# Moving the subtraction that makes a weight's low part from VectorE to GpSimd, in a one-core attention and feed-forward kernel

## The chip, the cores and the metric

The kernel runs on one core of one Trainium2 chip. The metric is the device time of one execution in microseconds. The engines are named as in the profile: PE is TensorE's matrix multiplication and PEld its weight load, DVE is VectorE, ACT is ScalarE, POOL is GpSimd and SP is SyncE, which here only issues DMAs.

## The reference

Eight batches of 448 tokens go through attention with 12 heads of 64 (q and k are first normalised by their root mean square and scaled by a gain), then through a two-dimensional Fourier transform whose real part is added to the input, and then through a feed-forward layer over 768 and 3072 columns. Cut to what is computed:

```python
q_n, k_n = rmsnorm(q, g_q), rmsnorm(k, g_k)
attn = softmax(q_n @ k_n.T / 8)
x = (attn @ v)                      # heads side by side: [8, 448, 768]
u = x + real(fft2(x))               # over tokens and columns
un = (u - mean(u)) / sqrt(var(u) + 1e-06)
out = u + relu(un @ w_ch1) @ w_ch2
```

The two weight matrices come as 64-bit floats; everything else is 32-bit.

## The kernel before, in words

PE multiplies numbers in a rounded 32-bit format (F32R in the code). To keep precision, an operand is held as two such numbers: a high part, which is the value rounded, and a low part, which is the value less its high part. A product of two split operands takes three passes.

`ffn` is the main stream: for each batch, `up(m)` multiplies with piece m of the first weight matrix (24 pieces of 6 blocks of 128x128, so 768 columns, tile h on line 992), and `down(g, d)` with piece (g, d) of the second one (36 pieces of 4 blocks, 512 columns, tile o on line 1013). The pieces' split form sits in tiles w, in two streams with three tiles each, which alternate in the first batch.

In the first batch no split form exists yet, and `convert` makes it from the 64-bit weights, once for each of the 60 pieces; afterwards the split form is stored to DRAM (line 793) and later batches only load it. Its steps for one piece, with the lines of the profile:

- line 746: SP loads the 64-bit words into a tile dbl (two buffers, which a few other tiles share).
- lines 749 and 750, ACT: the absolute value of each word's high half goes to a tile mag (two buffers); the low half is scaled in place.
- lines 751, 755 and 759, DVE: a clamp, a shift and a bit merge on mag, the last one with dbl as its second input.
- line 763, POOL: mag plus the low half of dbl, as 32-bit integers. It is the last reader of dbl.
- line 764, ACT: the rounded value goes to w's high part.
- line 765, DVE: mag less the high part goes to w's low part. It is the last reader of mag.

Fourteen of the pieces are converted early, while the attention of the first batches runs, and their tiles are called mage, dble, w1e and w2e; the other 46 are converted as the first batch's `ffn` comes to need them (mag, dbl, w).

Around this runs the side stream `aux`: attention of a batch (`transpose_pair`, `softmax_pair`, `value_pair`), the folding of its output for the Fourier transform (`fold`, tiles eo, sd and tot on DVE), the transform itself (`spectral`, tiles y, Y, ab, smdf, x and un). For the first batch it has PE to itself, for later ones it is merged into the `ffn` of the batch before. POOL's other work is a power of -1/2 on a small tile ss, which each head pair's normalisation waits for; a copy rs for the division by the softmax sums in the first two batches; the same power for rstd; and, from the third batch on, the squares qkn.

Each engine runs its instructions in order. That order is written by the framework's scheduler, which plans the whole program with its own estimate of each instruction's length; a change of one instruction's engine can so change the order on all of them. `behind` adds one rule: while the first batch's attention runs, a conversion step is placed no earlier than four recorded instructions back on its engine. Small operations that all go through one helper have its line, 114, so they are told apart by their tiles.

Of the kernel before, what the change touches and what calls it, by code (L numbers as in the profile page):

```python
# [11 lines left out]
F32 = mybir.dt.float32  # L12
# [4 lines left out]
ALU = mybir.AluOpType  # L17
# [73 lines left out]
def spectral_block(ctx, tc, q, k, v, g_q, g_k, w1, w2, d1, d2, out, nb=B):  # L91
    nc = tc.nc
# [30 lines left out]
    def order(ins, before, kind, reason):  # L123
        tc.add_manual_dep(
            ins.ins, before.ins.name, mybir.DependencyInfo(kind, reason),
            reason="issue order",
        )

    def behind(ins):

        others = given.get(ins.ins.engine, [])
        if starting[0] and len(others) > LAG:
            order(
                ins, others[-1 - LAG],
                mybir.DependencyClass.NoSync, mybir.DependencyReason.DATA,
            )
# [23 lines left out]
    def wide(name, dtype=F32):  # L160
        return sb.tile([128, 1800], dtype, tag="X", name=name, bufs=2)
# [576 lines left out]
    def convert(src, bits, part, name):  # L738

        _, c, f = src.shape
        raw = wide(f"dbl{name}", U32)[:, : c * f].rearrange(
            "r (c f w) -> r c f w", c=c, w=2
        )
        nc.sync.dma_start(raw.rearrange("r c f w -> r c (f w)"), src)
        low, high = raw[:, :, :, 0], raw[:, :, :, 1]
        value = bits.bitcast(F32)
        behind(nc.scalar.activation(value, high.bitcast(F32), AF.Abs))
        behind(nc.scalar.activation(low, low, AF.Copy, scale=2.0**-29))  # L750
        behind(nc.vector.tensor_scalar(
            out=value, in0=value, scalar1=MIN_HIGH, scalar2=MAX_HIGH,
            op0=ALU.max, op1=ALU.min,
        ))
        behind(nc.vector.tensor_scalar(
            out=bits, in0=bits, scalar1=5, scalar2=2,
            op0=ALU.logical_shift_left, op1=ALU.logical_shift_right,
        ))
        behind(nc.vector.scalar_tensor_tensor(  # L759
            out=bits, in0=high, scalar=0xC0000000, in1=bits,  # L760
            op0=ALU.bitwise_and, op1=ALU.bitwise_or,
        ))
        behind(nc.gpsimd.tensor_tensor(out=bits, in0=bits, in1=low, op=ALU.add))  # L763
        behind(nc.scalar.copy(part[0], value))
        behind(nc.vector.tensor_tensor(
            out=part[1], in0=value, in1=part[0], op=ALU.subtract
        ))

    early = set()
# [1 line left out]
    class Stream:  # L771
# [14 lines left out]
        def converted(self, p, name):  # L786
            hl = self.tile(p, name)
            n = hl.shape[2]
            bits = slot("M", f"mag{name}", U32)[:, : n * 128].rearrange(
                "r (c f) -> r c f", c=n  # L790
            )
            convert(piece_doubles(p), bits, [hl[:, k] for k in range(2)], name)
            nc.sync.dma_start(piece_kept(p), hl.bitcast(F32))
            return hl
# [314 lines left out]
```

## Time and profile before

| what | value |
|---|---|
| median of 3 runs | 2173.51 us |
| the runs | 2165.72, 2174.75, 2173.51 us |
| span of the profiled execution | 2158.8 us |
| its own device time | not listed apart; the lowest run is 6.9 us above the span |
| granted TensorE clock, mean over the span | 0.983 |
| PE, DVE, ACT, POOL busy | 2085.6, 1551.6, 1053.9, 343.4 us |

The span reaches from the first to the last instruction that the profile holds. The busy times are sums over the whole span; what they mean for one stretch is read from a table by stretches.

### The profile page before, as it was taken

What the parts mean: (1) busy time and instruction counts of PE and PEld (TensorE: products, weight loads), DVE (VectorE), ACT (ScalarE), POOL (GpSimd) and SP (SyncE); (2) the same over time, 40 slices, a digit from 0 to 9 for tenths busy, and PEclk for the clock granted to TensorE, in tenths of its full rate; (3) what the DMA queues carried; (4) which work ended last, traced back from release to release, by engine and by line L of the source; (5) the groups of instructions that cost most, each with busy time, mean ns of one, the idle gap of its engine ahead of it and who ended that gap; (6) DMA issues with size and microseconds to landing.
All of it is one profiled execution on the core that took longest, in us unless ns stands there. A gap on an engine that the chain in (4) does not pass through costs nothing.

```text
span 2158.8 us, 31384 instructions
## 1 busy us (share of the span) xinstructions
PE 2085.6 (97%) x11224; PEld 1858.1 (86%) x11224; DVE 1551.6 (72%) x3016; ACT 1053.9 (49%) x2258; POOL 343.4 (16%) x196
## 2 busy tenths in 40 slices
PE   7878999899999999999999999999999999999998
PEld 4557788788999999999999999999999989999998
DVE  7888788877885788758786688857787578754122
ACT  7967776455552555435552455425553355422100
POOL 4323334311110111001110011101110011000000
PEclk8977999999999999999999999999999999999999
DMA  5548877757555855667555666558556674458774
GB/s 172 181 125 272 257 249 255 243 200 214 170 167 182 238 180 168 175 206 225 161 176 177 215 197 176 171 190 239 171 165 188 204 209 142 150 175 251 234 248 150
DMA packets 294976, 424.79 MB, mean 197 GB/s; under 512 B 183283, under 2 KB 221156, under 8 KB 294820
## 3 DMA queue, kind: packets, MB, share of 16 engines
q1 hardware_dynamic: 290386, 420.67, 63.5%
q10 hardware_dynamic: 4434, 2.11, 0.4%
q8 instruction: 89, 1.46, 0.3%
q14 instruction: 67, 0.55, 0.1%
HBM read 362.53 MB, written 65.31 MB: 198 GB/s over the span
## 4 chain that ended last, share of the span: by engine, by line
PE 77%; DMA 3%; DVE 3%; ACT 1%; issue 1%; POOL 0%; DVEq 0%; SPq 0%; POOLq 0%; ACTq 0%
PE h L992 28%; PE o L1013 28%; PE S L382 5%; PE av L492 4%; PE pt L480 4%; DMA dbl<-w 2%; PE y L617 1%; PE qk L334 1%; PE oT L949 1%; PE x L649 1%; PE un L861 1%; PE av L497 1%; PE ab L694 1%; PE rem L437 1%; DMA u_dram<-u 1%
## 5 line engine op out<-in xcount | busy, mean ns | idle before, releaser
L1013 PE MATMUL o<-hs,w 128*128 128x448 f32 x3456 | 793.2, 372 | 2.9 <-DVE rounded L114 0.9
L992 PE MATMUL h<-unT,w 128*128 128x448 f32 x3456 | 784.0, 371 | 1.0 <-DVE hs L114 0.6
L1013 PEld LDWEIGHTS o<-hs,w 128*128 128x128 f32 x3456 | 638.4, 188 | 60.5 <-issue 3.8
L992 PEld LDWEIGHTS h<-unT,w 128*128 128x128 f32 x3456 | 639.8, 189 | 57.5 <-issue 4.1
L114 ACT ACTIVATE P<-S,mn 112x448 f32<-112x448 f32 x384 | 243.9, 637 | 196.9 <-DVE mn L114 188.1
L114 DVE TENSOR_REDUCE mn<-S 112x1 f32<-112x448 f32 x384 | 233.8, 617 | 33.0 <-PE S L382 30.3
L114 ACT ACTIVATE hs<-h 128x448 fp32r<-128x448 f32 x192 | 104.4, 544 | 304.5 <-PE h L992 302.9
L114 DVE SCALAR_TENSOR_TENSOR hs<-h,hs 128x448 fp32r<-128x448 f32 x192 | 119.3, 621 | 149.3 <-ACT hs L114 147.3
L114 DVE TENSOR_TENSOR acc<-o,acc 128x448 f32<-128x448 f32 (+1 forms) x240 | 147.0, 613 | 81.8 <-PE o L1013 79.1
L114 POOL TENSOR_TENSOR qkn<-raw 112x1024 f32<-112x1024 f32 x36 | 69.2, 1924 | 677.4 <-PE qk L334 391.5
L114 POOL TENSOR_TENSOR ss<-ss,nhalf 112x16 f32<-112x16 f32 x48 | 143.6, 2992 | 205.6 <-DVE ss L114 183.6
L382 PE MATMUL S<-KD,QT 128*112 128x448 f32 x384 | 152.8, 400 | 18.5 <-ACT KD L114 15.6
L114 ACT CAST T<-pt 128x448 fp32r<-128x448 f32 x216 | 112.9, 533 | 101.5 <-PE pt L480 97.9
L492 PE MATMUL av<-T,vhl 128*128 128x448 f32 x432 | 154.2, 385 | 0.8 <-DVE T L114 0.8
L114 DVE TENSOR_TENSOR T<-pt,T 128x448 fp32r<-128x448 f32 x216 | 131.7, 617 | 25.7 <-ACT T L114 24.7
L382 PE MATMUL S<-rounded,QT 128*112 128x448 f32 x384 | 143.7, 376 | 0.0
L114 DVE TENSOR_SCALAR P<-P,sm 112x448 f32<-112x448 f32 x288 | 122.7, 465 | 3.9
L480 PE MATMUL pt<-ident,P 112*128 112x112 f32 x864 | 122.1, 258 | 0.0
L480 PEld LDWEIGHTS pt<-ident,P 112*128 112x128 f32 x864 | 102.7, 140 | 15.8
L763 POOL TENSOR_TENSOR mag<-mag,dbl 128x512 uint32<-128x512 uint32 (+1 forms) x46 | 77.6, 1686 | 170.3 <-DVE mag L759 115.2
L114 POOL TENSOR_TENSOR rstd<-st,nhalf 112x1 f32<-112x1 f32 (+2 forms) x32 | 18.2, 570 | 505.7 <-DVE st L114 500.1
L382 PEld LDWEIGHTS S<-KD,QT 128*112 128x112 f32 x384 | 68.5, 179 | 29.4 <-ACT KD L114 18.7
(116 smaller groups left out, 2528.3 us busy)
## 6 DMA issues: line engine op xcount, KB each, us to landing
w<-w SPq DMA_DIRECT2D x192, 768.0 KB, 5.4
w<-w SPq DMA_DIRECT2D x288, 512.0 KB, 4.5
dbl<-w SPq DMA_DIRECT2D x28, 512.0 KB, 5.3
dbl<-w SPq DMA_DIRECT2D x18, 768.0 KB, 5.1
raw<-q SPq DMA_DIRECT2D x96, 112.0 KB, 3.9
raw<-k SPq DMA_DIRECT2D x96, 112.0 KB, 4.0
v<-v SPq DMA_DIRECT2D x96, 96.0 KB, 3.6
u_dram<-u SPq DMA_DIRECT2D x24, 336.0 KB, 3.1
```

The costliest lines, as they stand in the source:

```text
L114: ins = emit(*args, **kwargs)
L334: nc.tensor.transpose(pt[:, c * C : (c + 1) * C], qk[:, i, c].rearrange("t h d -> t (h d)"), ident[:C, :C],)
L382: ins = nc.tensor.matmul(s_, QT[:, h, cs], K[:, h], start=step == 0, stop=step == 1)
L437: nc.tensor.transpose(rem[:, c * C : (c + 1) * C], Pc[c][:, 384:512], ident[:C, :C])
L480: nc.tensor.transpose(pt[:, c * C : (c + 1) * C], Pc[c][:, 512 * h + j * 128 : 512 * h + (j + 1) * 128], ident[:C, :C],)
L492: nc.tensor.matmul(av[:, :S], lv, T[:, i], start=(j == 0 and i == 0), stop=False)
L497: nc.tensor.matmul(av[:, :S], lv, R[:, h], start=False, stop=True)
L617: nc.tensor.matmul(o, src[:, par, t0 : t0 + n], D1[:, ri, par, cols], start=i != 1, stop=i != 0,)
L649: nc.tensor.transpose(xp[:n, i * 128 : (i + 1) * 128], src[:, 3 * half + i], ident)
L763: behind(nc.gpsimd.tensor_tensor(out=bits, in0=bits, in1=low, op=ALU.add))
L992: pace(nc.tensor.matmul(o, w[:, a, c], unT[c][:, z], start=n == 0, stop=n == 17))
L1013: pace(nc.tensor.matmul(o, w[:, a, f], hs[4 * g + f][:, z], start=n == 0, stop=n == 11))
```

## The change

The subtraction on line 765 is issued to GpSimd. Its second input is read as a plain 32-bit float; the numbers are the same bits.

```diff
--- before.py
+++ after.py
@@ -762,8 +762,8 @@
         ))
         behind(nc.gpsimd.tensor_tensor(out=bits, in0=bits, in1=low, op=ALU.add))
         behind(nc.scalar.copy(part[0], value))
-        behind(nc.vector.tensor_tensor(
-            out=part[1], in0=value, in1=part[0], op=ALU.subtract
+        behind(nc.gpsimd.tensor_tensor(
+            out=part[1], in0=value, in1=part[0].bitcast(F32), op=ALU.subtract
         ))
 
     early = set()
```

The order of instructions moves on all engines from here to the middle of the second batch. Three places follow; lines with - stand only before, with + only after the change.

The first is on DVE, where the first batch's last head pair is divided (xT), the second batch's scores are reduced (mn) and its queries are split (QT). The tiles mage4_1 and w1e4_1 belong to the early piece (4, 1).

```order
 L755 TENSOR_SCALAR mage4_1_1274<-mage4_1_1274 128x512
+L759 SCALAR_TENSOR_TENSOR mage4_1_1274<-dble4_1_1275,mage4_1_1274 128x512
 L114 TENSOR_REDUCE mn1_0_0_1262<-S1_0_0_1_1264 112x1
-L759 SCALAR_TENSOR_TENSOR mage4_1_1274<-dble4_1_1275,mage4_1_1274 128x512
 L114 TENSOR_REDUCE mn1_0_1_1312<-S1_0_1_0_1313 112x1
-L765 TENSOR_TENSOR w1e4_1_1273<-mage4_1_1274,w1e4_1_1273 128x512
 L114 TENSOR_REDUCE mn1_0_1_1312<-S1_0_1_1_1314 112x1
+L114 TENSOR_TENSOR QT1_1_1434<-qk1_1_0_1436,QT1_1_1434 64x448 x2
+L114 TENSOR_REDUCE mn1_0_2_1371<-S1_0_2_0_1372 112x1
 L114 TENSOR_TENSOR xT0_295<-rt0_5_1388,xT0_295 128x448
```

The subtraction has left DVE's queue, the bit merge stands one reduction earlier, and the split of QT has moved ahead of the division.

The second is on DVE too, where the first batch's normalised rows are split for `ffn` (unT) and its first pieces are converted.

```order
 L114 SCALAR_TENSOR_TENSOR u0_3_1581,st0_3_1582<-x0_111_1588,smdf0_1_1547 112x384
+L114 TENSOR_SCALAR st0_3_1582<-st0_3_1582 112x1
 L751 TENSOR_SCALAR mag_0_1_1627<-mag_0_1_1627 128x768
-L114 TENSOR_SCALAR st0_3_1582<-st0_3_1582 112x1
 L755 TENSOR_SCALAR mag_0_1_1627<-mag_0_1_1627 128x768
 L759 SCALAR_TENSOR_TENSOR mag_0_1_1627<-dbl_0_1_1628,mag_0_1_1627 128x768
-L751 TENSOR_SCALAR mag_0_2_1640<-mag_0_2_1640 128x768
 L114 TENSOR_SCALAR st0_1_1564<-st0_1_1564 112x1
-L755 TENSOR_SCALAR mag_0_2_1640<-mag_0_2_1640 128x768
-L759 SCALAR_TENSOR_TENSOR mag_0_2_1640<-dbl_0_2_1641,mag_0_2_1640 128x768
 L114 TENSOR_TENSOR unT0_0_1685<-un0_0_1680,unT0_0_1685 128x448
```

Three conversion steps of piece 2 have gone from ahead of unT to behind it.

The third is on POOL, in the first batch's `ffn`, at pieces (2, 3) and (2, 4) of the second matrix; ss1_5 is the power for the second batch's last head pair.

```order
+L763 TENSOR_TENSOR mag_0_2_3_2837<-mag_0_2_3_2837,dbl_0_2_3_2838 128x512
+L763 TENSOR_TENSOR mag_0_2_4_2885<-mag_0_2_4_2885,dbl_0_2_4_2886 128x512
+L765 TENSOR_TENSOR w1_0_2_3_2836<-mag_0_2_3_2837,w1_0_2_3_2836 128x512
 L114 TENSOR_TENSOR ss1_5_3045<-ss1_5_3045,nhalf_73 112x16
-L763 TENSOR_TENSOR mag_0_2_3_2837<-mag_0_2_3_2837,dbl_0_2_3_2838 128x512
-L114 COPY rs1_2_2899<-sums1_2_2138 112x512
-L763 TENSOR_TENSOR mag_0_2_4_2885<-mag_0_2_4_2885,dbl_0_2_4_2886 128x512
+L765 TENSOR_TENSOR w2_0_2_4_2884<-mag_0_2_4_2885,w2_0_2_4_2884 128x512
```

The power ss1_5 now stands behind two integer additions and one subtraction, of which it stood ahead before; and a subtraction stands between one piece's addition and the next.

## Rows read from the trace of the kernel before

**Rows 1.** The page's head, and part 1: busy time, share, instructions of each engine.
```profile
span 2158.8 us, 31384 instructions
PE 2085.6 (97%) x11224; PEld 1858.1 (86%) x11224; DVE 1551.6 (72%) x3016; ACT 1053.9 (49%) x2258; POOL 343.4 (16%) x196
```

**Rows 2.** Busy time by stretches; the first row names the columns.
```profile
core 0: us, PE busy (x) PEld busy (x) DVE busy (x) ACT busy (x) POOL busy (x), PEclk, DMA share, GB/s
...
20.00:120.00 100.00, 80.58 (x394) 53.76 (x393) 90.11 (x154) 96.03 (x215) 40.28 (x22) 0.93 0.55 166
120.00:190.00 70.00, 47.70 (x208) 37.38 (x206) 59.66 (x116) 47.44 (x89) 21.32 (x14) 0.68 0.59 201
190.00:450.00 260.00, 247.05 (x1236) 206.57 (x1235) 213.56 (x345) 170.44 (x335) 95.83 (x56) 0.99 0.75 246
...
540.00:2158.00 1618.00, 1611.16 (x8891) 1476.93 (x8889) 1112.87 (x2238) 684.51 (x1503) 169.11 (x88) 1.00 0.63 190
```

**Rows 3.** PE's waits, 20 to 120 us: us in total, times, longest.
```profile
PE S L382 <- ACT KD L114: 9.2, 7, 3.5
```

**Rows 4.** PE's waits, 120 to 190 us.
```profile
PE un L861 <- ACT un L114: 5.0, 2, 3.6
...
PE ab L694 <- DVE smdf L114: 3.2, 1, 3.2
...
PE S L382 <- DVE QT L114: 2.6, 1, 2.6
```

**Rows 5.** PE's waits, 190 to 450 us.
```profile
PE y L617 <- DVE eo L114: 4.2, 1, 4.2
PE qk L334 <- DVE qkn L114: 2.3, 1, 2.3
```

**Rows 6.** Groups of line 765 on DVE: busy us, mean ns; idle before.
```profile
L765 DVE TENSOR_TENSOR w<-mag,w 128x512 fp32r<-128x512 f32 (+1 forms) x46 | 39.0, 848 | 7.0 <-ACT w L764 5.7 <-issue 1.0
L765 DVE TENSOR_TENSOR w2e<-mage,w2e 128x768 fp32r<-128x768 f32 (+1 forms) x7 | 5.8, 832 | 0.7 <-ACT w2e L764 0.7
L765 DVE TENSOR_TENSOR w1e<-mage,w1e 128x512 fp32r<-128x512 f32 (+1 forms) x7 | 5.3, 758 | 1.3 <-ACT w1e L764 1.3
```

**Rows 7.** POOL's groups; two lines in tile mag's view (min/median/max ns, first, last start).
```profile
L763 POOL TENSOR_TENSOR mag<-mag,dbl 128x512 uint32<-128x512 uint32 (+1 forms) x46 | 77.6, 1686 | 170.3 <-DVE mag L759 115.2 <-DMA w<-w 10.9 <-ACT mag L749 9.0
L114 POOL TENSOR_TENSOR qkn<-raw 112x1024 f32<-112x1024 f32 x36 | 69.2, 1924 | 677.4 <-PE qk L334 391.5 <-DMA w<-w 162.2 <-DVE hs L114 102.9
...
L763 POOL TENSOR_TENSOR mag<-mag,dbl x46: 1276/1540/2895, 159.3 to 447.0; 128x512 uint32<-128x512 uint32 x28, 128x768 uint32<-128x768 uint32 x18
L764 ACT CAST w<-mag x46: 603/622/865, 169.5 to 448.6; 128x512 fp32r<-128x512 f32 x28, 128x768 fp32r<-128x768 f32 x18
```

**Rows 8.** Line 755 in the view of mag, and the timeline at 370 us.
```profile
L755 DVE TENSOR_SCALAR mag<-mag x46: 407/428/2250, 157.5 to 445.6; 128x512 uint32<-128x512 uint32 x28, 128x768 uint32<-128x768 uint32 x18
...
370.51 2.25 DVE L755 TENSOR_SCALAR mag<-mag 128x768 uint32<-128x768 uint32 x1
...
369.63 2.72 POOL L114 TENSOR_TENSOR qkn<-raw 112x1024 f32<-112x1024 f32 x1 [1.94 <-PE qk L334]
```

**Rows 9.** DVE's timeline (start, length, what, idle before) at four subtractions.
```profile
135.92 0.69 DVE L765 TENSOR_TENSOR w1e<-mage,w1e 128x512 fp32r<-128x512 f32 x1 [1.30 <-ACT w1e L764]
...
152.29 0.96 DVE L765 TENSOR_TENSOR w2e<-mage,w2e 128x768 fp32r<-128x768 f32 x1 [0.70 <-ACT w2e L764]
...
417.77 0.95 DVE L765 TENSOR_TENSOR w<-mag,w 128x768 fp32r<-128x768 f32 x1
...
423.36 0.94 DVE L765 TENSOR_TENSOR w<-mag,w 128x768 fp32r<-128x768 f32 x1
```

**Rows 10.** PE's first h; then one piece's subtraction and its first use on PE.
```profile
177.06 0.74 PE L992 MATMUL h<-unT,w 128*128 128x448 f32 x1
...
315.41 0.96 DVE L765 TENSOR_TENSOR w<-mag,w 128x768 fp32r<-128x768 f32 x1 [1.04 <-issue]
...
333.52 1.39 PE L992 MATMUL h<-unT,w 128*128 128x448 f32 x6
```

## The prediction

> **What bounds the kernel now.** I read the page's busy times first, then the table by stretches, then PE's waits in each stretch, and only then single lines.
>
> Over the whole span PE is busy 2085.6 of 2158.8 us [rows 1], so at most some 73 us can be won by anything but less work for PE. The table by stretches tells where they lie [rows 2]: behind 540 us PE is busy 1611 of 1618 us, and no conversion runs there. The change can act only on the 450 us in which weights are converted, and it shows at the end only as far as PE reaches the later work earlier or later. In that part there are three stretches with different limits.
>
> - 20 to 120 us: PE has 80.6 of 100 us, DVE 90.1, ACT 96.0 [rows 2]. ACT is the limit, and PE's longest list of waits, 9.2 us, is for ACT's KD [rows 3].
> - 120 to 190 us: PE has only 47.7 of 70 us and the granted clock is 0.68, between the two levels 1.2 and 2.4 GHz; ACT is at 47.4 and DVE at 59.7 [rows 2]. The first batch's transform is a chain from engine to engine here, and PE's waits are for DVE (smdf, QT) or for ACT's un [rows 4].
> - 190 to 450 us: PE has 247 of 260 us [rows 2]. What is left are two waits for DVE, 4.2 and 2.3 us [rows 5]. In none of the stretches does PE wait for a converted weight.
>
> **The change part by part.**
>
> *Off DVE.* 60 subtractions leave it: 39.0 + 5.8 + 5.3 = 50.1 us of busy time [rows 6]. Between 20 and 120 us this wins nothing that the rows show, since ACT is full and its three steps of a conversion stay. Between 190 and 450 us the cover is PE's own work, and without that cover nothing changes either, because weights are early: the subtraction that starts at 315.41 ends at 316.37 us, and PE first reads that piece (number 13, found by its place in the order) at 333.52, 17 us later [rows 10].
>
> What lies on the path are subtractions that stand right ahead of what PE waits for. I count four: the one at 135.92 us ahead of QT and xT, the one at 152.29 ahead of the second half of Y, and those at 417.77 and 423.36 inside the chain of folds that PE awaits for 4.2 us [rows 4, 5, 9]. Their busy times are 0.69 + 0.96 + 0.95 + 0.94 = 3.5 us. At the first two DVE also stood idle for ACT's cast, 1.30 and 0.70 us [rows 9], and this goes with them, which makes 5.5 us. Some of it is another engine's wait anyway; I take 5.
>
> *On to POOL.* The price of a 32-bit float subtraction of this shape on POOL does not appear before the change. The nearest row is line 763, the same shapes with two inputs: 1.69 us on average [rows 7]. The other end is the float product qkn, 1.924 us for 1024 columns; at that rate the 36 pieces of 512 and 24 of 768 columns, 36,864 columns in all, take 69 us. I take line 763, 60 x 1.69 = 101 us, since its operands are alike and qkn reads one input twice. Between 190 and 450 us POOL is busy 95.8 of 260 us [rows 2]; some 43 pieces add 73, which gives 65%. POOL is far from full.
>
> *Given back by blocking.* An instruction of DVE can be held up by one of POOL: line 755 takes 0.43 us as a rule and 2.25 us at 370.51, where it ends just behind POOL's qkn, at 372.76 against 372.35 us [rows 8]. So the move does not free DVE of the whole 50 us. Bounds: nothing, if no new subtraction meets such an instruction; 60 x 0.84 = 50 us, if every one of them holds up one for half its length. I take the middle way for the four places: POOL's busy share rises from 37% to 65%, so an instruction of this kind is caught 28 points more often, for 0.84 us each time, which is 0.24 us; about two of them lie on the path at each place, 8 x 0.24 = 1.9 us.
>
> The Trainium skill ("SBUF — State Buffer", section "Who interferes with whom") says that GpSimd and VectorE share one pair of ports, that whoever comes first has it for the whole instruction while the other fully blocks, and that this strikes VectorE's instructions with two inputs in SBUF and its two-port modes, but not reductions. The end of line 755 just behind POOL's agrees with it; what it would make of the time is the second rival.
>
> *Order of POOL's queue.* The subtraction waits for ACT's cast (line 764), and behind it in POOL's queue stand the next piece's addition, which frees the load buffer, and the small power that each head pair's normalisation needs. In the first 190 us each such power stands behind a cast that was over, by the trace of before, when the power could start. The one exception that I found is ss1_5, which slides behind two additions and a subtraction; PE does not wait for that pair's transposes before, its one wait for qkn being another pair's [rows 5]. I cost the order at 0, as long as casts come within 2 us (first rival). Bounds: 0 and the 30 us worked out there. Moves of the order on PE and ACT I cannot price one by one; a place gained here is lost there, and I give them 5 us in both directions.
>
> *Sum.* -5 + 1.9 = -3.1 us, say -3. The profiled execution would come to 2155.8 us of span. The lowest run is 6.9 us above that span and the median 14.7, so I put the difference on the median: 2173.5 - 3 = 2170.5 us.
>
> **The rivals.** 0.5% of the time, 10.9 us, is about what a measurement of this kernel can tell from no change.
>
> 1. *POOL's queue becomes the conversion's pace (slower).* The 46 later pieces start between 159.3 and 447.0 us, one in 6.4 us [rows 7]. With the subtraction in POOL's queue a piece occupies it in series: addition 1.69, the wait for the cast and the cast itself (0.6 to 0.8 us), subtraction 1.69, together 4.1 us [rows 7], or 4.6 with a tenth for POOL's other work. That leaves 1.8 us for casts that come late. Where they are later on average, PE outruns the weights; at 2.5 us the surplus of 0.7 us on 46 pieces is 32 us, of which the lead of some 17 us [rows 10] can hide a part. Against it: the additions can still run ahead of the subtractions at about a third of the pieces. Price +15 to +30, about 2195 us; chance 0.14.
> 2. *Blocking eats the gain.* If every subtraction on POOL meets one of DVE's instructions, the 50 us removed return as 50 us of waits, and at the four places 0.84 us for each of the four and the same again for their neighbours is 6.7 us against 5. Price 0 to +5: 2174 to 2178 us, in which the change would not be seen. For it speaks that the folds and bit steps next to the path are of the kind that is held up. Chance 0.30, which includes that the change simply lies beside other work.
> 3. *DVE is the limit more widely than I think (faster).* If the whole of the first 190 us hangs on DVE, the 20 subtractions in it give all their time, 20 x 0.83 = 16.6 us, less a fifth for blocking, 13 us, and with the folds later 15 us: 2158 us. Against it speaks ACT at 96 of 100 us. Chance 0.16.
>
> **How the numbers follow.** The forecast has 0.40 for itself: -8 to +2 us around 2170.5. Beside it stand 0.30 for the second rival, 0.16 for the third and 0.14 for the first. The range from 2155 to 2186 takes in the third rival's price and the light half of the first one's, and leaves out about 0.07 above and 0.08 below. Faster by more than 10.9 us is the third rival alone, 0.16; slower by more than that the first, 0.14; the rest, 0.70, is within.
>
> **What would show it.** Line 765 should appear on POOL at 1.3 to 2.1 us, POOL's busy time should rise by about 100 us and DVE's fall by 30 to 45, not by 50. From 20 to 120 us ACT should still be at about 96. PE's wait for QT [rows 4] should shrink by a microsecond, and the one for eo [rows 5] by one or two. Behind 540 us all should be the same. A line in PE's waits that names w with line 765 or 764 would show the first rival; lines 751, 755 or the folds with means up by a half the second; a DVE that no longer shows 8 to 9 tenths before 190 us, with PE ahead by over 10 us there, the third. The prediction is wrong if PE starts its first h more than 8 us earlier or later than at 177.06 us [rows 10], or if it loses or wins more than 8 us between 190 and 450 us.

## The result, and the profile after

The changed kernel takes 2185.18 us (median of 4 runs, 2183.22 to 2188.87), the kernel before beside it 2169.61 (2163.20 to 2174.75). The ratio is 1.0083, 95% interval [1.0064, 1.0102]: slower by 15.6 us of the medians, more than the 0.5% that I had set as the bound, where I had forecast 3 us less. The two profiled executions lie further apart (span 2187.1 against 2158.8 us), since that of after is the longest of its four and that of before is shorter than any of its four runs; the sizes below are taken from ratios, the places from traces.

The page's head and part 1, after, to be held against [rows 1]:

```profile
span 2187.1 us, 31351 instructions
PE 2094.1 (96%) x11224; PEld 1860.9 (85%) x11224; DVE 1540.4 (70%) x2956; ACT 1053.2 (48%) x2258; POOL 434.0 (20%) x256
```

POOL has 91 us more, and DVE, from which 50.1 us of subtractions were taken [rows 6], has only 11 us less. So some 39 us came back on DVE in instructions that did not change. The table by stretches, after, with the columns of [rows 2]:

```profile
20.00:120.00 100.00, 80.67 (x373) 52.46 (x373) 87.63 (x143) 93.25 (x212) 53.93 (x30) 0.91 0.55 163
120.00:190.00 70.00, 45.48 (x221) 36.05 (x220) 51.82 (x104) 44.40 (x85) 31.23 (x20) 0.76 0.55 183
190.00:450.00 260.00, 238.16 (x1144) 196.13 (x1142) 198.32 (x284) 166.46 (x324) 152.01 (x93) 0.97 0.73 238
540.00:2187.00 1647.00, 1634.64 (x9007) 1495.95 (x9005) 1127.30 (x2271) 695.13 (x1529) 169.12 (x88) 1.00 0.63 189
```

Between 190 and 450 us PE is busy 238 us where it had 247, and gets through 1144 instructions where it had 1236. That is where the time is lost. From a place at 190.5 us of before (192.0 after) to one at 441.1 us (461.3) PE does the same 1188 instructions; they take 250.6 us before and 269.3 after, of which PE stands idle 12.7 and 24.6 us. The granted clock in these stretches is 0.99 and 0.97, which comes to about 5 us of the difference (0.02 of 269 us, an estimate). So some two thirds of the loss are waits, and most of the rest goes with the lower clock. PE's first h comes 3.5 us later than in [rows 10]:

```profile
180.57 0.74 PE L992 MATMUL h<-unT,w 128*128 128x448 f32 x1 [1.56 <-ACT unT L114]
```

At places of PE's program where both orders have done the same instructions, PE is 6 us behind at 210 us, 9 at 322, 16 at 373 and 21 at 441, and no conversion runs after that. PE's longest waits from 190 to 480 us, after, are for DVE and ACT, and none of the waits is put down to a converted weight w:

```profile
PE o L1013 <- DVE acc L114: 4.9, 2, 3.4
PE av L456 <- ACT T L114: 4.3, 7, 1.1
PE y L617 <- DVE eo L114: 3.9, 1, 3.9
PE qk L334 <- DVE hs L114: 3.4, 1, 3.4
```

The last of these rows is new, and the first was next to nothing before:

```profile
PE o L1013 <- DVE acc L114: 0.5, 1, 0.5
```

The timeline around the longest wait for acc (start, length, what; in brackets the idle time before and its releaser) shows what happened:

```profile
387.31 1.88 POOL L765 TENSOR_TENSOR w<-mag,w 128x768 fp32r<-128x768 f32 x1 [1.81 <-ACT w L764]
387.42 2.18 DVE L751 TENSOR_SCALAR mag<-mag 128x768 f32<-128x768 f32 x1
...
389.14 2.21 POOL L114 TENSOR_TENSOR qkn<-raw 112x1024 f32<-112x1024 f32 x1
...
389.52 2.85 DVE L114 TENSOR_TENSOR sd<-eo 128x450 f32<-128x450 f32 x2
...
393.84 0.61 DVE L114 TENSOR_TENSOR acc<-o,acc 128x448 f32<-128x448 f32 x1
...
394.51 1.92 PE L1013 MATMUL o<-hs,w 128*128 128x448 f32 x7 [3.44 <-DVE acc L114]
```

Line 751 starts 0.11 us behind POOL's subtraction and ends 0.4 us behind its end: 2.18 us for what takes 0.56 undisturbed (the group of 768 columns in the trace of before: 558 ns). The next two, 1.24 us as a rule, run beside POOL's qkn and take 2.85. The addition into acc, which reads a tile o of PE's and so frees its place for the next one, stands behind both, and PE waits 3.44 us.

To count this I compared every DVE instruction with the median of its like (same line, tiles and shape) that overlap nothing of POOL's, where there are at least two of them. More than 0.15 us over it were 33 instructions before, by 29.5 us together, and 54 after, by 62.5 us together. I call this the **held time** below. The groups on DVE that gained most, first before, then after (busy us, mean ns):

```profile
L759 DVE SCALAR_TENSOR_TENSOR mag<-dbl,mag 128x768 uint32<-128x768 uint32 x18 | 17.2, 957 | 0.3
L755 DVE TENSOR_SCALAR mag<-mag 128x512 uint32<-128x512 uint32 x28 | 13.4, 478 | 0.6
L114 DVE TENSOR_TENSOR qkn<-raw,ss 112x512 f32<-112x512 f32 x96 | 65.9, 725 | 10.1 <-POOL ss L114 9.6
```

```profile
L759 DVE SCALAR_TENSOR_TENSOR mag<-dbl,mag 128x768 uint32<-128x768 uint32 x18 | 24.1, 1337 | 0.3
L755 DVE TENSOR_SCALAR mag<-mag 128x512 uint32<-128x512 uint32 x28 | 22.7, 812 | 0.6
L114 DVE TENSOR_TENSOR qkn<-raw,ss 112x512 f32<-112x512 f32 x96 | 73.1, 800 | 8.0 <-POOL ss L114 7.6
```

On POOL the subtraction costs what line 763 does [rows 7], and line 763 itself got cheaper (its 512-column group; before 1468 ns):

```profile
L765 POOL TENSOR_TENSOR w<-mag,w 128x512 fp32r<-128x512 f32 x28 | 41.1, 1472 | 27.6 <-ACT w L764 22.0 <-PE qk L334 5.7
L763 POOL TENSOR_TENSOR mag<-mag,dbl 128x512 uint32<-128x512 uint32 x28 | 36.9, 1316 | 44.6 <-DVE mag L759 27.4 <-DMA v<-v 5.0 <-PE S L382 4.5
L765 POOL TENSOR_TENSOR w<-mag,w 128x768 fp32r<-128x768 f32 x18 | 36.0, 2000 | 18.9 <-ACT w L764 11.2 <-DVE mag L755 4.4 <-DMA w<-w 3.3
```

### The profile page after: what moved, and what is told of

Read it like the earlier page. It is cut to its first block, busy times and chain, and to the rows that moved or that the text cites. A ratio compares the mean times of both kernels' runs of the same rounds, so it can differ in the third digit from the quotient of the medians.

```text
span 2187.1 us, 31351 instructions
## 1 busy us (share of the span) xinstructions
PE 2094.1 (96%) x11224; PEld 1860.9 (85%) x11224; DVE 1540.4 (70%) x2956; ACT 1053.2 (48%) x2258; POOL 434.0 (20%) x256
## 4 chain that ended last, share of the span: by engine, by line
PE 72%; DMA 6%; DVE 5%; issue 2%; POOL 2%; ACT 1%; SPq 0%; DVEq 0%; POOLq 0%; ACTq 0%
PE h L992 27%; PE o L1013 26%; PE S L382 5%; PE av L492 4%; PE pt L480 4%; DMA dbl<-w 2%; DMA u_dram<-u 2%; PE y L617 1%; DMA w<-w 1%; PE qk L334 1%; POOL mag L763 1%; DMA ur<-u_dram 1%; PE oT L949 1%; PE av L497 1%; DVE mag L759 1%
## 5 line engine op out<-in xcount | busy, mean ns | idle before, releaser
L114 DVE TENSOR_TENSOR T<-pt,T 128x448 fp32r<-128x448 f32 x216 | 131.6, 617 | 24.6 <-ACT T L114 23.4
L763 POOL TENSOR_TENSOR mag<-mag,dbl 128x512 uint32<-128x512 uint32 (+1 forms) x46 | 71.5, 1555 | 77.2 <-DVE mag L759 48.7
```

Of the source, the lines that this page charges most:

```text
L114: ins = emit(*args, **kwargs)
```

## The experiments

The experiments weigh four theories, and a fifth that came up on the way. **A**: blocking; POOL's subtraction holds up DVE's instructions. **B**: the new order that the scheduler made for the changed program. **C** (later **Q**): POOL's in-order queue; what stands behind the new instructions is late. **D**: the two mag buffers, which a piece lets go of later, so that line 749 on ACT and line 751 on DVE wait at the head of their queues. **S**: the store of the converted weight waits longer in SP's queue.

To keep B out, nearly all kernels below have the order of before, instruction by instruction, for the part in which weights are converted, forced by a table of instruction numbers; only new instructions are placed freely among them. All ratios are to the kernel before, each against runs on the same chip.

| run | what differs from before | ratio, 95% interval | held time, us |
|---|---|---|---|
| the change | | 1.0083 [1.0064, 1.0102] | 62.5 |
| e1 | subtraction on POOL, old order | 1.0067 [1.0054, 1.0080] | 60.4 |
| e2 | subtraction on DVE, new order | 1.0066 [1.0053, 1.0080] | 33.1 |
| e3 | POOL makes 8 of 128 columns | 1.0007 [0.9998, 1.0015] | 29.1 |
| e4 | POOL makes it too, unused | 1.0259 [1.0244, 1.0274] | 55.1 |
| e5 | POOL and mag held by a power | 1.0069 [1.0052, 1.0086] | 29.5 |
| e6 | three mag buffers | 0.9984 [0.9973, 0.9995] | 30.2 |
| e7 | e1 with three mag buffers | 1.0066 [1.0051, 1.0080] | 62.3 |
| e8 | 14 early pieces on POOL | 1.0001 [0.9990, 1.0013] | 35.4 |
| e9 | e5 with three mag buffers | 1.0027 [1.0017, 1.0036] | 30.6 |
| e10 | e4 with three mag buffers | 1.0153 [1.0136, 1.0170] | 60.5 |
| e11 | low part zeroed on DVE | 0.9973 [0.9961, 0.9984] | 24.8 |
| e12 | e11, POOL and mag held | 1.0006 [0.9997, 1.0016] | 27.5 |
| e13 | e12 with three mag buffers | 0.9996 [0.9986, 1.0005] | 28.9 |
| e14 | e12, store waits for POOL and memset | 1.0128 [1.0110, 1.0147] | 23.1 |
| e15 | e1, power and memset for the subtraction | 1.0077 [1.0064, 1.0090] | 32.4 |
| e16 | POOL subtracts a tile of its own | 1.0102 [1.0086, 1.0118] | 55.9 |
| e17 | POOL raises a tile of its own to a power | 1.0003 [0.9994, 1.0012] | 25.2 |
| e18 | e1, stores later in SP's queue | 1.0127 [1.0110, 1.0144] | 57.9 |

The held time has two levels: 55 to 63 us wherever POOL subtracts 512 or 768 columns for each of the 60 pieces, 23 to 35 us elsewhere. It does not go with the ratio alone: e2, e5, e14 and e15 lose as much as e1 or more on the lower level. The kernels e11 to e15 leave the low part of the weights out, e14 with wrong numbers in a few of its columns; only their times are used.

**e1 and e2: the engine or the order?**

```diff
+ORDER = {"PE": "128-135 159-162 ...", "DVE": ..., "Activation": ..., "Pool": ..., "SP": ...}
+def in_order(nc, tc):
+    for text in ORDER.values():
...
+                tc.add_manual_dep(ins, last, mybir.DependencyInfo(
+                    mybir.DependencyClass.NoSync, mybir.DependencyReason.DATA),
+                    reason="issue order")
```

e1 is the changed kernel with the table of the old order (without the 60 subtractions), e2 the kernel before with the table of the new one. e1:

> The subtraction runs on GpSimd as in the change, but every other instruction stands in exactly the order that it had before on PE, DVE, ACT, POOL and SP; only the 60 subtractions are new in POOL's order. Theory A (blocking: POOL's and DVE's instructions with SBUF inputs hold each other up) and theory C (POOL's in-order queue: the subtraction's wait for ACT's cast delays what stands behind it) both expect the slowdown of the change to stay: a ratio to the kernel before of 1.005 to 1.011. Theory B (the order that the scheduler made for the changed kernel is the worse one) expects it gone: 0.996 to 1.001, with the 3 us won that I forecast.

e2:

> The subtraction stays on VectorE, but every other instruction stands in exactly the order of the changed kernel on all five engines. Theory B (order) expects the slowdown here: 1.005 to 1.011. Theories A (blocking) and C (POOL's queue) expect none: 0.998 to 1.002.

Measured: 1.0067 and 1.0066. Each of them alone costs as much, and both together, the change, hardly more. e1 says that the slowdown needs no new order: with the old one PE works through the same list, and the instruction that before ended at 185.8 us ends 2.5 us later, the one that ended at 475.2 us 15.5 us later. So B is not needed for the result; what the new order adds to the move, 1.0083 against 1.0067, can't be told from nothing. That e2 loses as much was expected by B alone, and B is right so far: an order made for a subtraction on POOL is 14 us worse for one on DVE.

**e3 and e4: a little of POOL, and POOL beside DVE.** e3:

```diff
-            out=part[1], in0=value, in1=part[0], op=ALU.subtract
+            out=part[1][:, :, 8:], in0=value[:, :, 8:], in1=part[0][:, :, 8:], op=ALU.subtract
+        behind(nc.gpsimd.tensor_tensor(
+            out=part[1][:, :, :8], in0=value[:, :, :8],
+            in1=part[0][:, :, :8].bitcast(F32), op=ALU.subtract))
```

> The order of before on all engines; VectorE subtracts columns 8 to 127 of each block of 128, GpSimd the first 8 of each (32 or 48 columns of a piece). So POOL's queue gets the 60 waits for ACT's cast, as in the change, but only some 0.2 to 0.4 us of work for each. Theory C (queue) expects most of the slowdown: 1.004 to 1.010. Theory A (blocking) expects about a tenth of it or a little more, since so little of POOL's time is added: 0.999 to 1.002. Theory B (order) 0.999 to 1.001.

Measured 1.0007 [0.9998, 1.0015]: waiting for the cast in POOL's queue costs nothing by itself, with only a short step behind it; C falls in this form. e4:

```diff
+        for k in range(0, c, 4 if c == 4 else 1):
+            at = slice(k, k + (4 if c == 4 else 1))
+            behind(nc.gpsimd.tensor_tensor(out=spare, in0=value[:, at],
+                in1=part[0][:, at].bitcast(F32), op=ALU.subtract))
```

> The order of before on all engines; VectorE still makes the low part that is used, and GpSimd makes the same subtraction once more into columns that nobody reads (the pieces of 768 columns in six parts of 128). No weight waits for POOL. Theory A (blocking) expects VectorE to be held up as in the change but without the 50 us taken off it: some 35 us more of VectorE's time against before, and a ratio of 1.008 to 1.018. Theory C (queue) expects 1.004 to 1.010, theory B (order) 0.999 to 1.001.

Measured 1.0259, more than A expected. ACT's waits (20 to 480 us) tell why: the six small parts keep the mag buffer for too long, so this run mixes A with D.

```profile
ACT mag L749 <- POOL mag L770: 47.4, 13, 6.8
```

**e5 to e7, e9 and e10: the mag buffers.** A power of a few columns takes POOL long and touches little (2992 ns for the 16 columns of ss before). e5:

```diff
+        n = 7 if c == 4 else 10
+        behind(nc.gpsimd.tensor_tensor(out=spare[:, :n],
+            in0=part[0][:, 0, :n].bitcast(F32), in1=nhalf[:, :n], op=ALU.pow))
```

> The order of before on all engines; VectorE makes the whole low part. Behind each piece's cast GpSimd raises 7 (pieces of 512 columns) or 10 (768) columns to a power into spare columns of the same mag buffer, some 1.5 to 2.2 us of POOL for each: POOL's queue and the mag buffer are held about as long as by the subtraction of the change, but VectorE is hardly disturbed (in the trace of before the powers of ss held up none of the 237 instructions of DVE that they overlapped). Theory A (blocking) expects 0.999 to 1.002. Theory D (the two mag buffers: a piece lets go of its buffer later, so ACT's line 749 of the next piece but one, and DVE's line 751 behind it, stand at the head of their queues for longer) expects most of the slowdown of the first experiment: 1.004 to 1.010.

Measured 1.0069, and the held time is that of before, 29.5 us. D, it seemed, was enough for the whole loss. ACT's wait at line 749, in e5:

```profile
ACT mag L749 <- POOL mag L769: 28.9, 17, 2.8
```

So a third buffer was tried, first for the kernel before (e6), then for e1 (e7):

```diff
-    SLOTS = {"P": 8, "PT": 6, "M": 2, "unT": 6, "h": 6}
+    SLOTS = {"P": 8, "PT": 5, "M": 3, "unT": 6, "h": 6}
```

> Control for the next run: the kernel before with three mag buffers instead of two, paid for with five PT buffers instead of six; the order of before on all engines. All theories expect 0.997 to 1.005; it is the base for the next one.

> The same three mag and five PT buffers and the same order, with the subtraction on GpSimd. Against the control with three buffers theory A (blocking) expects the full slowdown, a ratio of 1.005 to 1.008, theory D (the mag buffers) expects 0.998 to 1.002: with a third buffer the later release delays nobody.

Measured 0.9984 for e6 and 1.0066 for e7. In e7 ACT no longer waits for POOL at line 749, and the loss is all there; the held time is 62.3 us. D is not what the change pays. e9 and e10 are e5 and e4 with the third buffer:

> The fifth experiment (VectorE subtracts, GpSimd holds its queue and the mag buffer with a small power for as long as a subtraction) with three mag buffers and five PT buffers; the base is the control of the sixth, 0.998 of the kernel before. Theory D2 (the fifth one's loss came through the two mag buffers alone) expects it gone: 0.997 to 1.001 of before. Theory Q (POOL's queue: what stands behind the 60 new instructions is late, the additions and the small powers above all) expects it to stay: 1.004 to 1.009, and would then explain the seventh as well.

> The fourth experiment (both engines make the subtraction, POOL's result is read by nobody) with three mag and five PT buffers. Theory A (blocking) expects VectorE's instructions to be held up by 25 to 35 us more than in the control, and a ratio to before of 1.008 to 1.016: the loss of the seventh, plus what VectorE's own 50 us are worth. Theory Q expects the value of the ninth, plus a little for POOL's longer time. Were the fourth one's loss the mag buffers' alone, 0.998 to 1.003.

e9 fell to 1.0027, between the two theories. The third buffer takes 0.0016 off the kernel before too (e6), and against that base 0.0043 of e5's 0.0069 is still there, 6 to 12 us by the intervals: some two fifths of e5's loss were the mag buffers. The rest comes without blocking (held time 30.6 us, e6 has 30.2), without a wait of ACT for POOL at line 749, and without a store that waits for POOL. That leaves theory Q, here for a step of 1.8 us (7 columns) or 2.1 us (10) that stands behind the cast. e10 fell from 1.0259 to 1.0153, inside what A gave; its held time, 60.5 us, is no lower than e4's 55.1.

**e8: where?**

```diff
+        if name[0] == "e":
             behind(nc.gpsimd.tensor_tensor(
                 out=part[1], in0=value, in1=part[0].bitcast(F32), op=ALU.subtract))
+        else:
+            behind(nc.vector.tensor_tensor(out=part[1], in0=value, in1=part[0], op=ALU.subtract))
```

> The order of before; only the 14 early conversions subtract on GpSimd, the 46 later ones on VectorE. In the first experiment PE was 2 to 3 us behind at 190 us and 15 us behind at 490 us, so by both A and D the early pieces cost little: 1.000 to 1.003. A ratio over 1.004 would say that the loss is made early and only shows later.

Measured 1.0001. The 14 early pieces cost nothing and bring nothing that this can tell (0.13%); what is lost is lost by the 46 later ones.

**e11 to e13: what the relief of DVE is worth, and the price without blocking.** e11, and what e12 adds to it:

```diff
-        behind(nc.vector.tensor_tensor(
-            out=part[1], in0=value, in1=part[0], op=ALU.subtract
-        ))
+        behind(nc.vector.memset(part[1].bitcast(F32), 0.0))
...
+        n = 5 if c == 4 else 8
+        behind(nc.gpsimd.tensor_tensor(out=spare[:, :n],
+            in0=part[0][:, 0, :n].bitcast(F32), in1=nhalf[:, :n], op=ALU.pow))
```

> The order of before. The low part is left out: instead of the subtraction VectorE fills it with zeros by a memset, and GpSimd does nothing in its place. This is the change without any price, as far as the memset is shorter than the subtraction (I expect 0.3 to 0.5 us instead of 0.69 to 1.02, so 20 to 35 us of DVE less). My prediction's step (the 50 us are worth 5) expects 0.997 to 0.999; if VectorE's time is worth more than I thought, as the difference between the seventh and the tenth hints, 0.990 to 0.996.

> The order of before. The low part is left out as in the eleventh (memset on VectorE), and GpSimd stands behind each cast for about as long as for the subtraction of the change, but with a small power (5 or 8 columns, some 1.5 and 1.9 us), which holds its queue and the mag buffer and disturbs VectorE hardly. So this is the change without the blocking. Theory A (blocking is what costs) expects 0.997 to 1.002, clearly under the 1.0067 of the first experiment. If POOL's queue and the two mag buffers are what costs, 1.004 to 1.009, as in the fifth.

> The twelfth experiment (low part left out, filled with zeros by VectorE; GpSimd holds its queue with a small power behind each cast) with three mag and five PT buffers. It tells the two halves of the 7 us between the eleventh and the twelfth apart. If they are the two mag buffers, the ratio falls to about that of the eleventh, 0.996 to 0.999; if they are POOL's queue, it stays at 0.999 to 1.002.

In e11 DVE's two large groups of line 765 are:

```profile
L765 DVE MEMSET w<- 128x512 f32 x28 | 13.6, 485 | 1.6
L765 DVE MEMSET w<- 128x768 f32 x18 | 12.6, 698 | 2.0
```

A memset fills a tile with a constant; here it also has no cast to wait for. With the early pieces the memsets take 34.2 us where the subtractions took 50.1: 15.9 us off DVE, with no price on POOL, bring 0.9973 [0.9961, 0.9984], 3 to 8 us. e12 gives this back (1.0006), and stays 0.6% under e1, though POOL is busy 418 us in it and 428 in e1. e13 is 0.0010 lower than e12, no more than a third buffer gives the kernel before. Its 0.9996 is what was expected if the 7 us between e11 and e12 are POOL's queue and not the mag buffers; with e9 this is the second sign that a step behind the cast costs something there. By the groups of line 759, e12's DVE is not disturbed, where e1's is; first e12, then e1:

```profile
L759 DVE SCALAR_TENSOR_TENSOR mag<-dbl,mag 128x512 uint32<-128x512 uint32 x28 | 20.0, 714 | 0.4
```

```profile
L759 DVE SCALAR_TENSOR_TENSOR mag<-dbl,mag 128x512 uint32<-128x512 uint32 x28 | 25.3, 903 | 0.6
```

This looked like A. But in e12 the store of a weight doesn't wait for POOL either, and in e1 it does.

**e14, e15 and e18: the chain from cast to store.** e14 lets POOL's power read mag and write into the low part that DVE's memset has filled:

```diff
+        link = nc.gpsimd.tensor_tensor(out=part[1][:, 0, :n], in0=value[:, 0, :n],
+            in1=ident[:, :n], op=ALU.pow)
+        order(link, cast, mybir.DependencyClass.Sync, mybir.DependencyReason.DATA)
```

> As the twelfth (order of before, low part left out and filled with zeros by VectorE's memset), but GpSimd's small power now reads the mag buffer and writes 5 or 8 columns of the low part itself, behind the cast. So the store of the converted weight, the DMAs behind it in SP's queue, PE's use of the weight and the mag buffer all wait for GpSimd as in the first experiment; only the two-input subtraction over the whole piece is missing. Theory A (blocking is what the first has over the twelfth) expects the twelfth's value, 0.999 to 1.003. Theory S (what the twelfth left out is SP's queue: stores that wait longer hold up the loads behind them) expects most of the first one's loss, 1.004 to 1.007.

Measured 1.0128, above both theories, with the lowest held time of all, 23.1 us. The run was not what it was meant to be, since the power had to wait for the memset too, but it shows that a longer chain can cost more than the change with less blocking than before. POOL's queue stands longer in it too, so it does not tell the two apart. SP's wait for the stored weight, 20 to 480 us, in e1 and in e14 (in the trace of before the like row is 71.6 us, for DVE):

```profile
SPq L793 <- POOL w L765: 88.5, 39, 7.2
```

```profile
SPq L801 <- POOL w L768: 130.1, 43, 8.4
```

e15 puts the zeroing on POOL, so that DVE is fully relieved:

```diff
-        behind(nc.gpsimd.tensor_tensor(
-            out=part[1], in0=value, in1=part[0].bitcast(F32), op=ALU.subtract
-        ))
+        n = 4 if c == 4 else 6
+        behind(nc.gpsimd.tensor_tensor(out=part[1][:, 0, :n], in0=value[:, 0, :n],
+            in1=part[0][:, 0, :n].bitcast(F32), op=ALU.pow))
+        behind(nc.gpsimd.memset(part[1].bitcast(F32), 0.0))
```

> The first experiment (order of before, VectorE relieved of the whole subtraction, the weight, its store and the mag buffer wait for GpSimd) with another operation on GpSimd: the low part is left out, and in its place stand a power of 4 or 6 columns behind the cast and a memset of the piece to zero, together some 1.5 to 2.2 us, about as long as the subtraction. VectorE and SP have the same work and the same waits as in the first experiment; only the reading of two whole operands is missing. Theory A (blocking makes the difference between the twelfth and the first) expects 0.996 to 1.002. Theory S (the longer waits of SP's stores, and of the mag buffer, make it) expects 1.004 to 1.009, the first one's value.

Measured 1.0077, S's value, with a held time of 32.4 us. POOL's two steps for a piece of 512 columns in e15, and behind them SP's waits for the store (line 796 here):

```profile
L766 POOL TENSOR_TENSOR w<-mag,w 128x4 fp32r<-128x4 f32 x28 | 31.4, 1122 | 24.1 <-ACT w L764 24.0
L770 POOL MEMSET w<- 128x512 f32 x28 | 14.7, 526 | 1.1
```

```profile
SPq L796 <- POOL w L770: 84.7, 37, 6.8
...
SPq L796 <- ACT w L764: 30.9, 18, 6.6
```

1.12 and 0.53 us are 0.26 more than e1's subtraction (1389 ns in the same shape), and the last row, in e1 0.4 us, is new, so e15 overstates the chain. Against e12, where POOL stands behind the cast too but no store waits for it, e15 loses 0.0071 more, some 15 us, with less work on DVE (1513.2 us busy against 1538.3). e18 is e1 with each store two transfers later in SP's table. A piece of SP's order, e1 with -, e18 with +:

```
-L793 DMA w_5_83<-w2e_385 128x1536
 L746 DMA dble_682<-w 128x6x256
 L204 DMA d2s<-d 112x452
+L793 DMA w_5_83<-w2e_385 128x1536
 L204 DMA d2s<-d 1x452
```

> The first experiment (subtraction on GpSimd, the order of before elsewhere) with one thing moved: each store of a converted weight stands two transfers later in SP's queue, behind loads that do not need it. Theory S (the stores' longer wait for GpSimd holds up the loads behind them, and this makes the first one's loss) expects 0.998 to 1.003. Theory A (blocking, which by the sixteenth and seventeenth is enough for it) expects 1.004 to 1.008, little less than the first one's 1.0067.

Measured 1.0127, worse than e1; both theories missed. SP's wait for line 763's buffers, now ahead of the stores, is 147.1 us in e18 against 101.7 in e1: the stores stand behind loads that wait for a later piece. That a later store goes with a loss fits S; that the loads behind it are the reason is not shown, since in e18 the order of the loads has changed as well.

**e16 and e17: blocking by itself.** Both kernels have the same instructions in the same places and give up the same PT buffer, DVE makes the low part, nothing waits for what POOL adds, and that waits for nothing but POOL:

```diff
-        x = beside[:, : 6 if c == 4 else 9]
-        more = nc.gpsimd.tensor_tensor(out=x, in0=x, in1=ident[:, : 6 if c == 4 else 9], op=ALU.pow)
+        x = beside[:, : c * (f // 2)]
+        more = nc.gpsimd.tensor_tensor(out=x, in0=x, in1=x, op=ALU.subtract)
         behind(more)
```

The lines with - are e17, those with + e16. e16:

> VectorE makes the low part as before, in the order of before. Behind each addition (line 763) GpSimd subtracts a tile of its own from itself, with 512 or 768 columns, for which one PT buffer of six is given up: two whole operands in SBUF are read for some 1.4 to 2.0 us, but nothing waits for the result, and it waits for nothing but POOL. To be compared with the next run, which has the same instructions in the same places. Theory A expects 1.006 to 1.016, and 0.004 to 0.010 more than the next run; theory S and theory Q expect the next run's value.

e17:

> The same as the run before it, instruction by instruction in the same order, but GpSimd raises 6 or 9 columns of its own tile to a power instead of subtracting 512 or 768: its queue is held about as long, VectorE is not disturbed. Theory A expects 0.999 to 1.004, theory Q (POOL's queue alone) 1.004 to 1.010 and no difference from the run before it.

Measured 1.0102 and 1.0003, with intervals far apart. POOL's added groups, first e16, then e17:

```profile
L773 POOL TENSOR_TENSOR beside<-beside 128x512 f32<-128x512 f32 x36 | 46.5, 1291 | 0.0
L773 POOL TENSOR_TENSOR beside<-beside 128x768 f32<-128x768 f32 x24 | 41.0, 1708 | 0.0
```

```profile
L773 POOL TENSOR_TENSOR beside<-beside,ident 128x6 f32<-128x6 f32 x36 | 56.0, 1555 | 0.0
L773 POOL TENSOR_TENSOR beside<-beside,ident 128x9 f32<-128x9 f32 x24 | 51.3, 2139 | 0.0
```

The power occupies POOL 20 us longer than the subtraction and costs nothing: theory Q falls for a step that waits for nothing. For one that waits for the cast, as the change's does, e9 and e12 stand against that. The subtraction costs 21 us of the kernel's time (1.0102 less 1.0003, of 2163), with 30.7 us more held on DVE. Blocking alone is thus enough for a loss larger than the change's, at a DVE that still has its own subtraction.

## Why the prediction was wrong

Step by step:

- **Off DVE, worth 5 us.** Not what failed: the relief is real, and 15.9 us of it bring 3 to 8 us (e11). The full 50 us may be worth well more than my 5; no run shows them without a price. That 20 to 120 us has little to give agrees with ACT's 93 us there, and with e11, where PE ends the instruction that before ended at 186 us 0.8 us later, not earlier.
- **On to POOL, 101 us.** Right: 1.47 and 2.00 us for the large groups, as line 763 before.
- **Given back by blocking, 1.9 us.** This is the step that failed. The mechanism was named and the row for it was there [rows 8], but I counted it at four places on the path only, as eight times 0.24 us. The trace of after has 33 us more held time, and e16 against e17 prices such blocking at 21 us. The error was to look for blocked instructions next to PE's waits of before. PE now waits for acc and hs, 4.9 and 3.4 us, where it waited 0.5 us and not at all: the timeline shows an instruction held for 1.6 us that delays what stands behind it in DVE's queue. DVE's total is a poor measure of this: e12 and e1 have the same DVE busy time, 1538.3 and 1540.1 us, and differ by 0.6%, though not by blocking alone, since in e12 no store waits for POOL. That what went was work with slack, and part of what came back stands ahead of urgent work, fits the traces but no run shows it by itself.
- **Order of POOL's queue, 0 us.** This failed as well. The wait alone (e3) and the length alone (e17) cost nothing, but a step of the subtraction's length behind the cast costs some 7 us with hardly more blocking than before (e12 against e11), and the first rival named that series of steps. And I asked for nothing that waits for the subtraction's result. The low part is finished 0.7 to 1.0 us later, its store waits longer in SP's queue (89.2 us after, 71.6 before, in the rows of line 793), and the mag buffer is let go of later. e15 loses 0.77% with hardly more blocking than before, and its stores are the main thing that it has over e12. These are terms that I had at nothing; what each is worth in the change no run shows.
- **Order on PE and ACT, 5 us either way.** It is not contradicted by the change: e1 with the old order and the change with the new one are not told apart. For other combinations it was too small, as e2 shows.
- **Rivals.** The first (weights too late for PE) is not seen as a lack of weights: PE's waits name no w. The second had the mechanism, with a price of 0 to 5 us that took DVE's waits to be no more than what had left; its upper end should have been the time of all of DVE's queue behind a held instruction. The third is not seen: the change is slower, and neither e8 nor e11 puts PE ahead by 186 us.
- **What would show it.** POOL's rows and ACT's 93 came as said; DVE fell by 11 us, not by 30 to 45; the first h moved by 3.5 us, and 190 to 450 us lost some 19 (250.6 against 269.3 us for the same work), over the bound of 8 that I had set for being wrong. PE's wait for QT no longer stands among its waits from 120 to 190 us, and the one for eo shrank by only 0.3 us (4.2 to 3.9).

The Trainium skill ("SBUF — State Buffer", section "Who interferes with whom") says that a DVE instruction with two inputs in SBUF contends with a GpSimd instruction that reads SBUF but not with one that only writes it, that one in a two-port mode contends with GpSimd, and that the later one is blocked for the whole of the other. The timeline at 387 us agrees with it, for line 751 and for sd; so do the memsets of e15, which only write: of 19 overlaps with a single one of them four were held, by 1.3 us together, none of them with two inputs. The powers do not agree with it: they read SBUF and hold nothing in their 2992 ns (last section), and what was measured decides.

**What stays open**: how the change's 15.6 us divide. Blocking alone costs 21 us while DVE has its own subtraction too (e16, e17). A store that waits for POOL goes with a loss of 17 us net of DVE's relief, with hardly more blocking than before (e15), though its chain is longer than the change's. A step behind the cast in POOL's queue costs some 7 to 9 us (e12 against e11, e9 against e6). The change and e1 have all three and lose 14 to 18 us, so the three do not add up. No run takes one of them out of the change and leaves the others; e18, which was to, did not. Not needed for the loss are the new order (e1) and, for the subtraction, the scarce mag buffers (e7); POOL's occupancy by a step that waits for nothing costs nothing (e17).

The only version that beat the kernel before with its whole result is e6, three mag buffers for one PT buffer, at 0.9984 [0.9973, 0.9995]: some 3 us, and none of it has to do with the change.

## What to carry to other kernels

Before work is moved from VectorE to GpSimd, count how many of VectorE's instructions read two operands from SBUF or run long past their usual time beside GpSimd: a new GpSimd operation over whole tiles can hold such an instruction for up to its own length, and with it everything behind it in VectorE's queue (in e16 29 of 65 were held). Compare not only the time that leaves VectorE but what stands behind the instructions that are held: slack work that leaves may not pay for urgent work that comes late. And follow the moved result to all who wait for it, the store and the buffer as well as the consumer, and what stands behind its wait in GpSimd's queue.

## What was not expected of the hardware

- What holds VectorE is not how long GpSimd is busy but what it does. In the trace of before the powers of ss, 2992 ns each for 16 columns, overlap 237 DVE instructions and hold up none; in e17 123 overlaps with powers of 1.6 to 2.1 us held none, and in e16 29 of 65 overlaps with the subtractions were held, 19.0 us together (counted are instructions that overlap a single one of POOL's). Like against like: of the clamp and the shift on mag (lines 751 and 755 of before) 10 of 12 were held in e16 and none of 31 in e17.
- The order alone is worth as much as the change: e2 differs from the kernel before in nothing else and is 0.66% slower, with 33.1 us of held time against 29.5.
